# One batch of eight heads per unit, in place of four heads, in a cached-attention decode step beside an MLP

## The chip, the cores and the metric

The kernel runs on one core of one Trainium2 chip. The metric is the device time of one execution in microseconds (us), as a median over runs. A core has a matrix engine (TensorE, PE in the profile), a vector engine (VectorE, DVE), a scalar engine (ScalarE, ACT), GpSimd (POOL) and a queue engine (SyncE, SP) that here only issues transfers; 16 DMA engines carry every transfer. Tiles lie in SBUF, 128 partitions wide; TensorE writes its results to PSUM, from which VectorE or ScalarE copy them.

## The reference, cut to what matters

Eight batches, one query token each, width D = 448. Branch A is attention with 16 query heads over 8 cached key/value heads of width 256, on the last W = 1024 of 4096 cached rows; branch B is a layer norm and a two-layer MLP of width 1792. A sigmoid gate of x mixes them. All inputs are bfloat16.

```python
q = (x @ wq).reshape(B, Sq, Hq, Dh).transpose(0, 2, 1, 3)
k = jnp.repeat(k_cache[:, :, Sk - W:, :], rep, axis=1)      # rep = 2
v = jnp.repeat(v_cache[:, :, Sk - W:, :], rep, axis=1)
scores = jnp.einsum("bhqd,bhkd->bhqk", q, k) * (Dh ** -0.5)
o = jnp.einsum("bhqk,bhkd->bhqd", _softmax(scores), v)
a = o.transpose(0, 2, 1, 3).reshape(B, Sq, Hq * Dh) @ wo
h = _gelu(_layernorm(x) @ w1 + b1)
b = h @ w2 + b2
g = _sigmoid((x * gate_w).sum(-1, keepdims=True))
out = g * a + (1 - g) * b
```

The keys and values that are read make 33.6 MB each, `wq` and `wo` 3.7 MB each, `w1` and `w2` 1.6 MB each. Each byte is read once.

## The kernel before

**Units.** A unit is half a batch: four key/value heads, their eight query heads, 1024 rows, so 16 units (`NQ`). The keys of a unit are one 2 MB load into one slot of 16 KB per partition; so are its values.

**The plan of loads.** A list written out by hand (lines 151 to 172) gives the order of all large loads: the keys of unit 0 in two halves, `w1`, `wq` in two slots, `w2`, then keys and, three units behind (`LAG`), values in turn, and `wo` in two slots, whose last pieces are small (line 70). `pump` (95) issues them on SP's queue into a ring of nine slots (`RING`); `done` (101) frees a slot after the last matmul that reads it and issues the next load. A load also waits until the load eight before it has landed, since loads share eight semaphores.

**Order of the work.** No scheduler changes the order: every engine runs its instructions as the program lists them. For each unit `transpose_keys` (330) turns the keys on TensorE: 32 transposes of 128x128 words (two bfloat16 values moved as one float32), four to a PSUM tile of three buffers, each tile copied to SBUF in turn by ScalarE (349) or VectorE (351). Between these groups stand the softmax steps of the unit before (`steps`, 443): `expo` behind group 0, `turn` behind group 2, `bring` behind group 6. Then TensorE runs `values` of the unit three before (450), `scores` of this unit (391), VectorE takes the maximum (`top`, 405), and `finish` (476) of the unit three before follows.

- `scores` writes four heads to four strips of 32 partitions of `S_ps`; only eight rows of a strip are wanted, and of these two belong to the strip's own head.
- `expo` is the exponential with a row sum; `turn` a VectorE transpose of 32x32 blocks (423); `bring` two matmuls, one that permutes partitions (431) and one in float32 that spreads the sums (434).
- `values` multiplies two row chunks at a time into four strips of `PO`; VectorE adds the two chunks (465, 466).
- `finish` is two float32 matmuls (481) that add the strips, normalise and transpose at once, and a copy into `oT` (484).

**Ahead of the units** come the layer norm, the gate and their TensorE transposes (`norm_and_gate`, 272; `transposed`, 229), the MLP's first layer with the weights as the stationary operand (`mlp_hidden`, 488: 70 matmuls of eight columns), the queries (`query`, 356), and, after unit 0's scores, the second layer (`mlp_out`, 536: 60 matmuls of 112 columns in four strips). Small inputs come on ScalarE's queue (179 to 187), among them `gate_w` as a broadcast of eight rows and `b1` as 128 short rows.

**Behind the units**, `spread_rows` (584) moves the heads to the layout of `wo` with 32 small matmuls, `project` (599) multiplies with `wo` in 128 matmuls of 112 columns, one VectorE instruction (620) mixes the branches, and four DMAs, two on SP's and two on ScalarE's queue, write the output (630).

Of the kernel before, what the change touches and what calls it, by code (L numbers as in the profile page):

```python
# [17 lines left out]
def kernel(  # L18
# [15 lines left out]
    nc = tc.nc  # L34
# [10 lines left out]
    assert (NB, Sq, D, Hkv, Dh, Hq, W, F) == (8, 1, 448, 8, 256, 16, 1024, 1792)  # L45
    NJ = Dh // P
    NC = W // P
# [3 lines left out]
    NF = F // P  # L51
    FH = F // 2
    HH = HD // 2
    PAIR = 2
    OT = 4
    DO = D // OT
    QN = 512
    QUAD = 4
    RQ = QUAD * rep
    NQ = NB * Hkv // QUAD  # L60
    SK = P // QUAD
    NCK = W // SK
    NH = 2
    CH = NCK // NH
    SLOT = 8192
    CB = NC // NJ
    HPQ = 4
    NHQ = Hq // HPQ
    NJ8 = HPQ * NJ
    WO_PARTS = [[(0, NJ8)]] * (NHQ - 1) + [[(0, 4), (4, 6), (6, 8)]]  # L70
    RING = 9
    LAG = 3
    BIG = 1e30
# [8 lines left out]
    ktpool = ctx.enter_context(tc.tile_pool(name="ktpool", bufs=4))  # L82
    epool = ctx.enter_context(tc.tile_pool(name="epool", bufs=2))
    opool = ctx.enter_context(tc.tile_pool(name="opool", bufs=LAG + 1))
# [8 lines left out]
    consumed = [0]  # L93

# [10 lines left out]
    def kv_loader(src, u, parts):  # L105
        b, half = divmod(u, Hkv // QUAD)
        v = src[b, half * QUAD : (half + 1) * QUAD, kv_base:Sk, :].rearrange(
            "a (s c) d -> s a (c d)", c=NCK
        )

        def load(t):
            n = NCK * Dh // parts
            for i in range(parts):
                nc.sync.dma_start(  # L114
                    t[:, i * n : (i + 1) * n], v[:, :, i * n : (i + 1) * n]
                )

        return load

    def rows_loader(pieces):  # L120
        def load(t):
            o = 0
            for ap in pieces:
                n = 1
                for s in ap.shape[1:]:
                    n *= s
                dst = t[:, o : o + n]
                if len(ap.shape) == 3:
                    dst = dst.rearrange("p (a n) -> p a n", a=ap.shape[1])
                nc.sync.dma_start(dst, ap)  # L130
                o += n

        return load

    index = {}

    def add(key, loader):
        index[key] = len(plan)
        plan.append(loader)

    def add_kv(name, src, u, parts=1):
        add((name, u), kv_loader(src, u, parts))
# [5 lines left out]
    w2_v = B_w2.rearrange("(p c) n -> p (c n)", c=NF)  # L148
    wo_v = A_wo.rearrange("(q p j) n -> p q (j n)", p=P, j=NJ8)

    add_kv("k", A_k_cache, 0, parts=2)
    add(("w1",), rows_loader([w1_m, w1_t]))
    add(("wq", 0), rows_loader([wq_m[:, 0 : 2 * HD]]))
    add(("wq", 1), rows_loader([wq_m[:, 2 * HD : 3 * HD], wq_t]))
    add(("w2",), rows_loader([w2_v]))
    for u in range(1, NQ):
        add_kv("k", A_k_cache, u)
        if u >= LAG:
            add_kv("v", A_v_cache, u - LAG)
    for u in range(NQ - LAG, NQ):  # L160
        add_kv("v", A_v_cache, u)
    for q in range(0, NHQ, 2):
        add(
            ("wo", q),
            rows_loader(
                [
                    wo_v[:, q + i, j0 * D : j1 * D]
                    for i in range(2)
                    for j0, j1 in WO_PARTS[q + i]
                ]  # L170
            ),
        )

    def slot(*key):
        return slots[index[key]]

# [3 lines left out]
    gw_b = consts.tile([NB, D], BF16)  # L180
    b2_r = consts.tile([1, D], BF16)
    b1_sb = consts.tile([P, NF], BF16)
    nc.scalar.dma_start(
        gw_b[:], gate_w.rearrange("(o d) -> o d", o=1).to_broadcast([NB, D])
    )
    nc.scalar.dma_start(b2_r[:], B_b2.rearrange("(o d) -> o d", o=1))
    nc.scalar.dma_start(b1_sb[:], B_b1.rearrange("(p c) -> p c", c=NF))

# [4 lines left out]
    ones_f = consts.tile([P, P], F32)  # L193
    nc.gpsimd.memset(ones_f[:], 1.0)
# [3 lines left out]
    PO = ps_po.tile([P, PAIR, Dh], F32)  # L198
    nc.vector.memset(PO[:], 0.0)

    NX = NR + 2

    def tiles(ps):
        return [
            (ps[32 * i : 32 * i + NB, :], slice(i * DO, (i + 1) * DO))
            for i in range(OT)
        ]

    xz = consts.tile([NB, 2, P], BF16)
    yz = consts.tile([NB, 2, P], BF16)  # L210
    nc.vector.memset(xz[:], 0.0)
    nc.vector.memset(yz[:], 0.0)
    xT = consts.tile([P, NX, NB], BF16)
    yT = consts.tile([P, NX, NB], BF16)
    sel = consts.tile([P, RQ], F32)
    sel2 = consts.tile([P, RQ], F32)
    own = consts.tile([P, PAIR], F32)
    qw = consts.tile([P, NJ, NB, Hq // RQ, QUAD, RQ], BF16)
    oT = consts.tile([P, Hq, NJ, NB], BF16)
    gg = consts.tile([NB, 2], F32)  # L220
    spread = consts.tile([NB, OT, P // OT], F32)
    gg_s = consts.tile([P, 2], F32)
    ones_r = consts.tile([1, NB], BF16)
    mixb = consts.tile([P, DO], F32)
    res = consts.tile([P, DO], BF16)
    nc.vector.memset(spread[:], 0.0)
    nc.vector.memset(ones_r[:], 1.0)

    def transposed(dst, src, srcz):
        tp = ps_misc.tile([P, NX, NB], BF16, tag="misc", name="tp")  # L230
        for r in range(NR):
            nc.tensor.transpose(tp[:, r, :], src[:, r:DM:NR], ident[:NB, :NB])
        for h in range(2):
            nc.tensor.transpose(tp[:, NR + h, :], srcz[:, h, :], ident[:NB, :NB])
        nc.vector.tensor_copy(dst[:], tp[:])

    for h in range(2):
        nc.vector.tensor_copy(xz[:, h, h::2], x_sb[:, DM:D])
    transposed(xT, x_sb, xz)
    nc.vector.reduce_sum(  # L240
        sel[:], ident[:].rearrange("p (a s) -> p s a", a=QUAD)[:, 0:RQ, :], axis=AXIS.X
    )
    halfs = ident[:].rearrange("p (a s) -> p s a", a=QUAD)
    for i in range(PAIR):
        nc.vector.reduce_sum(
            own[:, i : i + 1], halfs[:, i * RQ : (i + 1) * RQ, :], axis=AXIS.XY
        )
    nc.vector.reduce_sum(
        sel2[:],
        ident[:]  # L250
        .rearrange("p (a h s) -> p s a h", a=QUAD, s=RQ)[:, :, :, 0:PAIR],
        axis=AXIS.XY,
    )
    perm = consts.tile([P, P], BF16)
    nc.vector.tensor_copy(
        perm[:].rearrange("p (s a) -> p s a", a=QUAD),
        ident[:].rearrange("p (a s) -> p s a", a=QUAD),
    )
    cap = consts.tile([P, 1], F32)
    rows = consts.tile([P, 1], F32)  # L260
    for a in range(QUAD):
        nc.vector.reduce_sum(
            rows[32 * a : 32 * a + 32, :],
            ident[32 * a : 32 * a + 32, (32 + rep) * a : (32 + rep) * a + rep],
            axis=AXIS.X,
        )
    nc.vector.tensor_scalar(
        cap[:], rows[:], 2.0 * BIG, -BIG, op0=ALU.mult, op1=ALU.add
    )
    nc.vector.memset(qw[:], 0.0)  # L270

    def norm_and_gate():
# [18 lines left out]
        for h in range(2):  # L291
            nc.vector.tensor_copy(yz[:, h, h::2], y_sb[:, DM:D])
        transposed(yT, y_sb, yz)
# [6 lines left out]
            in1=gw_b[:],  # L300
# [5 lines left out]
        nc.scalar.activation(gth[:], gl[:], ACT.Tanh, scale=0.5)  # L306
        nc.vector.tensor_scalar(
            gg[:, 0:1], gth[:], 0.5, 0.5, op0=ALU.mult, op1=ALU.add
        )
        nc.vector.tensor_scalar(  # L310
            gg[:, 1:2], gth[:], -0.5, 0.5, op0=ALU.mult, op1=ALU.add
        )
        nc.vector.tensor_copy(
            spread[:, :, 0:NB],
            ident[0:NB, 0:NB]
            .rearrange("p (o b) -> p o b", o=1)
            .to_broadcast([NB, OT, NB]),
        )
        gp = ps_misc.tile([P, 2], F32, tag="misc", name="gp")
        nc.tensor.matmul(  # L320
            gp[:],
            lhsT=spread[:].rearrange("p i b -> p (i b)"),
            rhs=gg[:],
# [3 lines left out]
        nc.vector.tensor_copy(gg_s[:], gp[:])  # L327

    KT = {}
    def transpose_keys(u, between=None):  # L330
        kn = slot("k", u)[:].bitcast(F32)
        between = between or {}
        for hf in range(NH):
            kt = ktpool.tile([P, QUAD, CH, SK, NJ], BF16, tag="kt", name="kt")
            KT[hf] = kt
            for i in range(CH // CB):
                c0 = i * CB
                g = hf * (CH // CB) + i
                ktp = ps_kt.tile([P, CB, P, NJ], BF16, tag="ktp", name="ktp")
# [12 lines left out]
                for step in between.get(g, ()):  # L352
                    step()
# [209 lines left out]
    for u in range(1, NQ):  # L563
        transpose_keys(u, steps(u - 1))
        if u >= LAG:
            values(u - LAG)
# [94 lines left out]
```

## Time and profile before

| | us |
|---|---|
| runs | 194.29, 194.04, 194.38 (median 194.29) |
| span of the profiled execution, first to last instruction | 192.9 |
| TensorE matmul busy | 141.4 (73%), 1478 matmuls and as many weight loads |
| VectorE busy | 121.4 (63%), 278 instructions |
| ScalarE busy | 84.3 (44%), 102 instructions |
| DMA | 77.90 MB in 6737 packets, mean 404 GB/s |
| mean granted TensorE clock | 0.907 |

How to read it. The profile is one execution; its span leaves out what lies around the first and last instruction, so the runs' median is 1.4 above it. The page cuts the span in 40 slices and gives each engine's busy share in tenths; PEclk is the clock granted to TensorE, and DMA the mean busy share of the 16 DMA engines. "The chain that ended last" goes back from the last instruction, at each step to what released it. A row of "groups" has the line, the engine, the operation, out<-in with shapes, the count, the busy time in all, the mean duration of one in ns, and the idle time of the engine before it with what ended most of that. A row of a timeline has start, duration, engine, line, operation, and in brackets the idle time before it and its releaser. A row of windows gives a stretch, its length, the busy time and count of PE, PEld (weight loads), DVE, ACT and POOL, then granted clock, DMA share and GB/s. Matmuls overlap, so the mean duration of one is more than the spacing between two.

### The profile page before, as it was taken

Reading aid. Unit: us, or ns where it says so; the run is one execution under the profiler, and the core shown is the slowest. Engines: PE = TensorE matmul, PEld = TensorE weight load, DVE = VectorE, ACT = ScalarE, POOL = GpSimd, SP = SyncE. Lnnn points to the kernel's source line nnn. Section 1 sums busy time; section 2 is a strip of 40 time slices with the busy share of each in tenths; the row PEclk is TensorE's granted clock in tenths of the full one; section 3 lists DMA queues with packets and bytes.
Section 4 is the critical chain, followed back from the end, with each engine's and each line's share of the span. In section 5 each row is a group of like instructions: output and inputs, shape, how many; then the busy total and the mean of one; then the engine's idle time right before and its main releaser. Section 6 shows DMA issues by size and latency. Waiting matters only on the chain.

```text
span 192.9 us, 3529 instructions
## 1 busy us (share of the span) xinstructions
PE 141.4 (73%) x1478; PEld 104.7 (54%) x1478; DVE 121.4 (63%) x278; ACT 84.3 (44%) x102; POOL 1.3 (1%) x9
## 2 busy tenths in 40 slices
PE   1299957788888859797858586869786978935671
PEld 0199526465575649484636363739473948612360
DVE  7632335797987848576858676765867584863310
ACT  2343024587583817182818182827282725520000
POOL 2000000000000000000000000000000000000000
PEclk9999699999999997969999999996999696995558
DMA  5999999999999999999999999999999999999960
GB/s 173 426 427 415 429 440 423 404 431 431 431 431 421 425 418 425 435 426 428 425 418 431 416 431 428 428 428 421 428 428 421 428 431 425 428 418 413 417 240 7
DMA packets 6737, 77.90 MB, mean 404 GB/s; under 512 B 945, under 2 KB 1346, under 8 KB 1986
## 3 DMA queue, kind: packets, MB, share of 16 engines
q1 hardware_dynamic: 6512, 77.67, 95.5%
q8 instruction: 11, 0.18, 0.4%
q10 hardware_dynamic: 210, 0.02, 0.2%
q14 instruction: 4, 0.03, 0.0%
HBM read 77.68 MB, written 0.01 MB: 403 GB/s over the span
## 4 chain that ended last, share of the span: by engine, by line
DMA 96%; SPq 1%; issue 0%; DVE 0%; PE 0%
DMA slot<-in_A_k_cache_dram 58%; DMA slot<-in_A_v_cache_dram 21%; DMA slot<-in_A_wo_dram 10%; DMA slot<-in_A_wq_dram 7%; SPq L114 1%; SPq L130 1%; DVE res L620 0%; PE A_ps L604 0%
## 5 line engine op out<-in xcount | busy, mean ns | idle before, releaser
L343 PE MATMUL ktp<-ident_f,slot 128*128 128x128 f32 x512 | 78.0, 306 | 24.3 <-DMA slot<-in_A_k_cache_dram 16.0
L349 ACT COPY kt<-ktp 128x1024 bf16<-128x1024 bf16 x64 | 63.2, 1016 | 71.2 <-PE ktp L343 71.1
L343 PEld LDWEIGHTS ktp<-ident_f,slot 128*128 128x128 f32 x512 | 64.7, 157 | 33.6 <-issue 16.2
L351 DVE COPY kt<-ktp 128x1024 bf16<-128x1024 bf16 x64 | 41.8, 686 | 27.5 <-PE ktp L343 27.5
L423 DVE STREAM_TRANSPOSE EB<-E 128x1024 bf16<-128x1024 bf16 x16 | 19.9, 1243 | 5.9 <-ACT E L415 5.9
L407 DVE TENSOR_REDUCE nmx<-S_ps 128x1 f32<-128x1024 f32 x16 | 19.5, 1219 | 3.3 <-PE S_ps L395 3.3
L456 PE MATMUL PO<-slot,ET 128*16 128x512 bf16 x256 | 18.3, 410 | 2.1 <-DMA slot<-in_A_v_cache_dram 2.1
L395 PE MATMUL S_ps<-kt,qw 128*8 128x512 bf16 x256 | 18.2, 388 | 1.4 <-ACT kt L349 1.1
L415 ACT ACTIVATE E<-S_ps,nmx 128x1024 bf16<-128x1024 f32 x16 | 17.9, 1119 | 2.4 <-DVE nmx L408 2.4
L395 PEld LDWEIGHTS <-qw 128*8 128x8 bf16 x256 | 7.1, 85 | 8.8 <-issue 2.1
L456 PEld LDWEIGHTS <-ET 128*16 128x16 bf16 x256 | 5.4, 91 | 8.7 <-issue 5.4
L436 DVE CAST ET<-sm 128x256 bf16<-128x256 f32 x16 | 6.6, 415 | 0.7 <-PE sm L434 0.7
L434 PEld LDWEIGHTS sm<-selr,ones_f 128*128 128x128 f32 x32 | 5.0, 198 | 0.6 <-issue 0.4
L484 DVE CAST oT<-sm 128x16 bf16<-128x16 f32 x16 | 3.5, 219 | 2.9 <-PE sm L481 2.9
L434 PE MATMUL sm<-selr,ones_f 128*128 128x8 f32 x32 | 4.8, 222 | 0.0
L431 PE MATMUL sm<-EB,perm 128*128 128x256 bf16 x16 | 4.5, 279 | 0.3 <-DVE oT L484 0.3
L604 PE MATMUL A_ps<-slot,oP 128*8 128x112 bf16 x128 | 3.5, 273 | 1.1 <-DMA slot<-in_A_wo_dram 1.1
L514 DVE TENSOR_TENSOR z<-hT,b_sb 128x112 f32<-128x112 f32 x1 | 0.3, 274 | 5.5 <-PE hT L504 5.5
L604 PEld LDWEIGHTS <-oP 128*8 128x8 bf16 x128 | 2.7, 114 | 1.8 <-issue 1.8
L415 ACT ACTIVATION_READ_ACCUMULATOR E<-S_ps,nmx 128x1 f32 x16 | 3.2, 202 | 0.0
L363 PE MATMUL S_ps<-slot,xT 128*8 128x512 bf16 x32 | 3.2, 576 | 0.0
L438 DVE RECIPROCAL rb<-sm 128x8 f32<-128x8 f32 x16 | 3.2, 198 | 0.0
(145 smaller groups left out, 82.5 us busy)
## 6 DMA issues: line engine op xcount, KB each, us to landing
slot<-in_A_v_cache_dram SPq DMA_DIRECT2D x16, 2048.0 KB, 38.1
slot<-in_A_k_cache_dram SPq DMA_DIRECT2D x15, 2048.0 KB, 37.5
slot<-in_A_wo_dram SPq DMA_DIRECT2D x3, 896.0 KB, 31.8
slot<-in_A_k_cache_dram SPq DMA_DIRECT2D x2, 1024.0 KB, 7.4
slot<-in_A_wq_dram SPq DMA_DIRECT2D x1, 2048.0 KB
slot<-in_B_w_dram SPq DMA_DIRECT2D x1, 1568.0 KB
slot<-in_B_w_dram SPq DMA_DIRECT2D x1, 1344.0 KB, 10.1
slot<-in_A_wq_dram SPq DMA_DIRECT2D x1, 1024.0 KB
```

The costliest lines, as they stand in the source:

```text
L343: nc.tensor.transpose(words[:, c, :, 0], kn[:, o : o + P], ident_f[:])
L349: nc.scalar.copy(dst, src)
L351: nc.vector.tensor_copy(dst, src)
L395: nc.tensor.matmul(S_ps[32 * a : 32 * a + RQ, hf * CH * SK : (hf + 1) * CH * SK], lhsT=qw[:, j, b, half, a, :], rhs=KT[hf][:, a, :, :, j], ...
L407: nc.vector.reduce_max(nmx[:], S_ps[:], axis=AXIS.X, negate=True)
L415: nc.scalar.activation(E[:], S_ps[:], ACT.Exp, bias=nmx[:], scale=1.0, accum_out=rowsum[:])
L423: nc.vector.transpose(EB[:].rearrange("p c r -> p (c r)"), E[:])
L431: nc.tensor.matmul(sm[:, 0:NCK, :], lhsT=perm[:], rhs=EB[:, :, 0:RQ], start=True, stop=True)
L434: nc.tensor.matmul(sm[:, NCK, :], lhsT=ones_f[:], rhs=selr[:], start=True, stop=True)
L436: nc.vector.tensor_copy(ET[:], sm[:, 0:NCK, :])
L456: nc.tensor.matmul(PO[32 * t : 32 * t + PAIR * RQ], lhsT=ET[:, PAIR * c : PAIR * (c + 1), :], rhs=vn[:, PAIR * c * Dh : PAIR * (c + 1) * D ...
L604: nc.tensor.matmul(dst, lhsT=oP[:, j, q, :], rhs=w[:, o + cols.start : o + cols.stop], start=(q == 0 and j == 0), stop=(q == NHQ - 1 and j ...
```

## The change

A unit becomes a whole batch: eight key/value heads, sixteen query heads. What follows from it:

- **Loads.** A slot holds 32 KB per partition and the ring four slots. Keys and values of a batch come as two 2 MB loads, heads 0 to 3 and 4 to 7. `wq` is one slot, `w1` and `w2` share one, `wo` is one. Order: keys 0, `wq`, `w1`/`w2`, keys 1, then values and keys in turn with values two places behind, values 6, values 7, `wo`.
- **Order of the work.** No softmax step stands between the transposes. A batch is `transpose_keys`, `scores`, `softmax`, `values` of the batch before, `bring`, `finish` of the batch before.
- **Scores.** The stationary operand has four columns, two heads' queries with zeros for the other, so that both halves of the batch add into one tile of 16 wanted rows.
- **Softmax.** The exponentials stay float32, the row sum is a 33rd block column, and one VectorE block turn of 1056 columns (397) brings both over. A stream shuffle copies the sums to all lanes of a block, a reciprocal and the gate follow, and one multiplication gives `EZ`. `bring` is one bfloat16 matmul; `ET` is spread with a mask.
- **Values.** 32 matmuls per batch; each reads a chunk of both halves.
- **Finish.** No matmuls: a block turn of 512 float32 columns out of PSUM and six small additions on VectorE write `oP` in the layout of `wo`.
- **Projections of x and y.** Transposes by VectorE block turns and copies. The activations are the stationary operand and the weights stream: 28 matmuls of 512 columns for the queries, 14 of 448 for the first MLP layer, which now comes after batch 0's softmax, and 14 of 448 for the second.
- **Small inputs.** `gate_w` and `b2` come as one row each, `b1` as four rows, in six DMAs of one row; stream shuffles spread them.
- **Output.** 16 projections of 448 columns, four additions into `acc`, 32 of 224 columns, three more additions, two output DMAs.

The built program has 2300 TensorE instructions for 2987. The bytes loaded are the same. Cut to its core, with the lines of the changed kernel:

```diff
-    RING = 9
-    LAG = 3
+    RING = 4                      # L69; SLOT = NG * HS, 32 KB per partition
+    EARLY = 16
...
+    add(("k", 0), kv_loader(A_k_cache, 0))                      # L141
+    add(("wq",), rows_loader([wq_m, wq_t]))
+    add(("w12",), rows_loader([w1_m, w1_t, w2_v]))
+    add(("k", 1), kv_loader(A_k_cache, 1))
+    for b in range(2, NB):
+        add(("v", b - 2), kv_loader(A_v_cache, b - 2))
+        add(("k", b), kv_loader(A_k_cache, b))
+    add(("v", NB - 2), kv_loader(A_v_cache, NB - 2))
+    add(("v", NB - 1), kv_loader(A_v_cache, NB - 1))
...
+    nc.scalar.dma_start(rows_r[0:1, 0, :], gate_w.rearrange("(o d) -> o d", o=1))
+    nc.scalar.dma_start(rows_r[0:1, 1, :], B_b2.rearrange("(o d) -> o d", o=1))
+    for t in range(QD):
+        nc.scalar.dma_start(
+            b1_r[BL * t : BL * t + 1, :],
+            B_b1[FQ * t : FQ * (t + 1)].rearrange("(o d) -> o d", o=1),
+        )
...
+    nc.vector.stream_shuffle(b1_b[:], b1_r[:], [0] * BL)        # L209
...
+        nc.vector.transpose(                                    # L243
+            xt[:].rearrange("p a i b -> p (a i b)"),
+            xs[:].rearrange("p a r d -> p (a r d)"),
+        )
...
+    def scores(b):                                              # L372
+        CQ = QN // SK
+        for n in range(W // QN):
+            for u in range(NG):
+                for j in range(NJ):
+                    for t in range(QD):
+                        nc.tensor.matmul(
+                            S_ps[BL * t : BL * t + UR, n * QN : (n + 1) * QN],
+                            lhsT=qw[:, j, b, t, rep * u : rep * u + UR],
+                            rhs=KT[u][:, t, n * CQ : (n + 1) * CQ, :, j],
...
+    def softmax(b):                                             # L389
+        nc.vector.reduce_max(nmx[:], S_ps[:], axis=AXIS.X, negate=True)
+        nc.scalar.activation(
+            E[:, 0:W], S_ps[:], ACT.Exp, bias=nmx[:], scale=1.0,
+            accum_out=E[:, W : W + 1],
+        )
+        nc.vector.transpose(EB[:].rearrange("p c r -> p (c r)"), E[:])
+        nc.vector.stream_shuffle(rs[:], EB[:, NCK, :], [0] * BL)
+        nc.vector.reciprocal(sc[:], rs[:, 0:UR])
+        nc.vector.tensor_scalar_mul(sc[:], sc[:], gall[:, b : b + 1])
+        nc.vector.tensor_tensor(EZ[:], EB[:, 0:NCK, 0:UR],
...
+    def bring(b):                                               # L412
+        nc.tensor.matmul(sm, lhsT=perm[:], rhs=EZ, start=True, stop=True)
+        nc.vector.tensor_tensor(ET, sm, mask, op=ALU.mult)
...
+    def values(b):                                              # L435
+        for c in range(NCK):
+            t = c % QD
+            nc.tensor.matmul(
+                PO[BL * t : BL * t + Hq],
+                lhsT=ET[:, c].rearrange("p u a r -> p (u a r)"),
+                rhs=vn[:, c],
...
+    def finish(b):                                              # L449
+        nc.vector.transpose(T[:], PO[:].rearrange("p u (e j) -> p u j e", j=J8))
+        for u in range(NG):
+            nc.vector.tensor_tensor(Y[:, :, u, :], T[0:64, ...], T[64:128, ...], op=ALU.add)
+        for i in range(QD):
+            nc.vector.tensor_tensor(oP[BL * i : BL * (i + 1), :, :, b], ..., op=ALU.add)
...
+    transpose_keys(0)                                           # L532
+    query()
+    scores(0)
+    softmax(0)
+    hs = mlp_hidden()
+    bring(0)
+    mlp_out(hs)
+    for b in range(1, NB):
+        transpose_keys(b)
+        scores(b)
+        softmax(b)
+        values(b - 1)
+        bring(b)
+        finish(b - 1)
...
+    values(NB - 1)
+    finish(NB - 1)
+    for c in range(EARLY):                                      # L555
+        nc.tensor.matmul(A1[BL * g : BL * g + NB, :], ...)
+    for g in range(QD):
+        nc.vector.tensor_tensor(acc[:], A1[BL * g : BL * g + NB, :], acc[:], op=ALU.add)
+    for c in range(EARLY, NCH):
+        mine, tile_, base = (side, A3, 2 * BL) if c in side else (main, A2, 0)
+        for h in range(2):
+            nc.tensor.matmul(tile_[base + BL * h : base + BL * h + NB, :], ...)
+        if c == side[-1]:
+            for h in range(2):
+                nc.vector.tensor_tensor(fin[BL * h : BL * h + NB, :], ..., op=ALU.add)
+    nc.vector.tensor_tensor(res, A2, fin, op=ALU.add)           # L589
+    nc.sync.dma_start(out_f[:, 0:HALF], res[0:NB, :])
+    nc.scalar.dma_start(out_f[:, HALF:D], res[BL : BL + NB, :])
```

## The prediction

> **What bounds the kernel now.** I read the page's slices first, then the chain that ended last, then the tail in order of time, then the rows of one batch.
>
> ```profile
> DMA  5999999999999999999999999999999999999960
> ...
> q8 instruction: 11, 0.18, 0.4%
> ...
> ## 4 chain that ended last, share of the span: by engine, by line
> DMA 96%; SPq 1%; issue 0%; DVE 0%; PE 0%
> ```
>
> The 16 DMA engines are full from slice 2 to slice 38, and 96% of the chain is loads: 77.9 MB set the end, and work on the engines counts only where it delays a load or lies behind the last one. The q8 line matters below: 11 packets of TensorE's own instructions, 16 KB each, ride on the same engines.
>
> The windows of the end (columns: stretch, length, busy per engine, granted clock, DMA share, GB/s):
>
> ```profile
> 184.00:185.00 1.00, 0.68 (x9) 0.69 (x13) 0.22 (x1) 0.00 (x0) 0.00 (x0) 0.50 1.02 396
> 185.00:186.00 1.00, 1.00 (x59) 1.00 (x61) 0.29 (x1) 0.00 (x0) 0.00 (x0) 0.50 0.70 267
> 186.00:187.00 1.00, 0.79 (x35) 0.54 (x24) 0.00 (x0) 0.00 (x0) 0.00 (x0) 0.50 0.46 162
> 187.00:188.00 1.00, 0.86 (x32) 0.72 (x32) 0.00 (x0) 0.00 (x0) 0.00 (x0) 0.62 0.14 52
> 188.00:189.00 1.00, 0.55 (x24) 0.36 (x24) 0.00 (x0) 0.00 (x0) 0.00 (x0) 1.00 0.05 20
> ```
>
> The share decays over 4 us: the engines do not finish together, and at 188.5 one of 16 is left. A load has landed only when its slowest engine has. The trace's semaphore increments (one per engine and load) show how this grew: 0.8 us between first and last engine at 20 us, 2.6 at 149, 3.4 at 155, 4.1 for the last values (176.4 to 180.5). Each instruction packet takes 1.03 to 1.23 us and its engine comes out about 1.6 us later. Packets 1 to 8 (20.7 to 133.8 us) each put back an engine that was at most 0.8 late; 9 and 10 (153.1, 169.2 us) hit engines already late, as if eight engines served them in turn.
>
> **Stream.** 2987 TensorE instructions made 11 packets, one per 272; 2300 make 8.5, so 8: no engine is hit twice, and the spread stays at 2.6. Further, the eight 896-byte rows of `gw_b` took 0.38 to 0.69 us on seven engines at 4.1 us, which is the 0.8 at the start; now it is one row. I take 2.2 at the end (between 1.8 and 2.6) for 4.15: 1.95 us earlier. The first keys come in rows of 16 KB at 0.614 us, not two of 8 KB at 0.32 each: 8 per engine, 0.2 us. Last values at 180.54 - 2.1 = 178.4, last `wo` piece at 189.40 - 2.1 = 187.3. Bytes stay the same.
>
> [...]
>
> **Tail.** Before, from the last values to the end:
>
> ```profile
> 180.54 1.89 PE L456 MATMUL PO<-slot,ET 128*16 128x512 bf16 x16 [0.23 <-DMA slot<-in_A_v_cache_dram]
> ...
> 189.40 0.27 PE L604 MATMUL A_ps<-slot,oP 128*8 128x112 bf16 x8 [0.31 <-DMA slot<-in_A_wo_dram]
> ...
> 189.72 0.33 DVE L620 SCALAR_TENSOR_TENSOR res<-A_ps,gg_s,mixb 128x112 bf16<-128x112 f32 x1 [4.07 <-PE A_ps L604]
> 190.09 0.71 SPq L630 DMA_DIRECT2D out_dram<-res  x2
> ```
>
> Now both halves of the batch wait for the last values. 32 matmuls at 1.89/16 are 3.8 at clock 0.50 (2.1 at full clock, from 1.04 for 16); I take 3.6, the clock returning near their end. `finish` on VectorE: block turn of 512 columns, scaled from 1.243 for 1024, 0.71; two adds of 64 and four of 32 by the 112-wide add's 0.274 (0.157 fixed, 0.117 streaming), with gaps 1.3: 2.0. First 16 projections 1.0. Four adds of 448 into `acc` at 0.62 + 0.04, each on the one before: 2.65. Two of 224 into `fin` 0.86, `res` 0.39. With 0.2 of handovers: 178.4 + 3.6 + 2.0 + 1.0 + 2.65 + 0.86 + 0.39 + 0.2 = 189.1, against 190.05: the VectorE adds, not the last load, end it. One output DMA per queue for two saves 0.36. Together -1.3. At full clock the last load binds, 187.3 + 0.4 + 0.39 = 188.1, so -2.3. The span is 192.9, the median 194.29, so 1.4 lies around the span; 193.0 to 192.0.
>
> **The chain of a batch.** Here the cover can go. Before, `expo`, `turn` and `bring` of one unit lay between the transposes of the next; now `softmax`, `bring`, `finish` stand in program order, and TensorE's next transposes wait behind `bring`, which waits for VectorE.
>
> ```profile
> L351 DVE COPY kt<-ktp 128x1024 bf16<-128x1024 bf16 x64 | 41.8, 686 | 27.5 <-PE ktp L343 27.5
> L423 DVE STREAM_TRANSPOSE EB<-E 128x1024 bf16<-128x1024 bf16 x16 | 19.9, 1243 | 5.9 <-ACT E L415 5.9
> L407 DVE TENSOR_REDUCE nmx<-S_ps 128x1 f32<-128x1024 f32 x16 | 19.5, 1219 | 3.3 <-PE S_ps L395 3.3
> L349 ACT COPY kt<-ktp 128x1024 bf16<-128x1024 bf16 x64 | 63.2, 1016 | 71.2 <-PE ktp L343 71.1
> L415 ACT ACTIVATE E<-S_ps,nmx 128x1024 bf16<-128x1024 f32 x16 | 17.9, 1119 | 2.4 <-DVE nmx L408 2.4
> ```
>
> One batch, from the first transpose. Sixteen groups of four transposes at 0.50, three PSUM buffers, ACT and VectorE evicting in turn (1.02, 0.69); VectorE's first eviction waits behind `ET` (512 wide, 0.69) and `finish` (2.0) until 2.65. Stepping the buffers gives 10.1. Scores 32 x 0.068 = 2.2, maximum 1.22, exp to the turn's start 1.24, turn of 1056 columns 1.28, four small operations 1.0 with gaps, `bring` and handovers 0.4: 17.4. TensorE rests 2.9 us in it behind `values`. What that does to the clock:
>
> ```profile
> 159.00:160.00 1.00, 0.00 (x0) 0.00 (x0) 0.00 (x0) 0.00 (x0) 0.00 (x0) 1.00 0.96 410
> 160.00:161.00 1.00, 0.90 (x6) 0.93 (x7) 0.00 (x0) 0.04 (x1) 0.00 (x0) 0.73 1.12 475
> 161.00:162.00 1.00, 1.00 (x7) 1.00 (x6) 0.24 (x1) 1.00 (x2) 0.00 (x0) 0.50 0.97 410
> ```
>
> After 1.94 us of rest the clock stood at 0.50 for 3 us, though at 90 to 130 us the same rest left it at 1.00. Half-clock transposes delay the fourth group by 0.3, the rest is hidden behind evictions: 17.7 at most, I take 17.5. A float32 turn, shuffles and a 72-row matmul have no row. If 4-byte turns took twice the bfloat16 row, the cycle would be 19.3; if the small operations overlapped, 17.0. I take the row's 1.28.
>
> [...]
>
> A batch's loads take 2 x 9.8 = 19.6 us (8.4 MB at 428 GB/s), so the engines catch up 2 us per batch, and must: they start late. VectorE reaches the first key evictions only after `norm_and_gate`, which now waits for the `b1` rows (six one-row DMAs, each packet taking turns with 0.61 us key packets: landing at 7 to 11 us) and turns 1280 columns (1.5): 16 to 20 us, for 11.7. Rest of `transpose_keys(0)` 8, query 3.5, scaling, turn and 32 copies into `qw` at 0.11 to 0.18, 6 to 8, scores and softmax 7, MLP 2.2 + VectorE 5.2 + 14 matmuls of 448 in one strip 3.3 to 4.9: batch 1 starts transposing at 52 to 58; I take 55. Batch 7's `ET` is then ready at 55 + 16.4 (no `finish` ahead in batch 1) + 6 x 17.5 + 1.0 = 177.4: just ahead of the values at 178.4. The `w1`/`w2` slot comes free at that start too; an issue needs 1.4 us to its first packet (0.73 to 2.16 at the beginning), and the 23.6 MB queued ahead run dry at 58.2 (as many had landed on the first engine of before at 58.7), so up to 56.8 the stream never stops. Slots of 4 MB otherwise come free 2 us or more ahead.
>
> **Rivals.**
> 1. The stream and the tail set the end (sum above): 192.9, own range 191.8 to 193.9. For: DMA at 1.00, catching up 2 us a batch. Chance 0.52.
> 2. Slower: the chain of a batch becomes the bound. It decides from the point where start + 16.4 + 6 cycles + 1.0 passes 178.4, 1 us from my sum; each 0.1 us of cycle then costs 0.6, each us of late start 1. Start 57.5, cycle 17.9: 182.3, so 3.9 over rival 1, 196.9. For: every step is serial, and VectorE's new forms are unmeasured. Against: 1.28 and 0.69 have close rows. Chance 0.31.
> 3. Fewer fetches do not shorten the stream, and only the longer tail is felt: values to `res` 10.7 for 9.5, less 0.36, +0.8: 195.1. Chance 0.09.
> 4. Rival 2 just begins and eats rival 1's gain: 194.3. Chance 0.08.
>
> **The numbers.** Rival 1's time is the forecast, 192.9. The range 191.7 to 197.5 reaches over rivals 1, 3, 4 and most of 2. Faster by over 0.2% (the smallest difference a measurement of this kernel tells from none): rival 1 and a share of 4, 0.54; within: 0.10; slower: 0.36.
>
> **What would show it.** Right: 8 instruction packets; last values within 2.6 us from first to last engine, landing near 178.4; `values` of batch 7 waiting for the load and not for `ET`; DMA share 1.00 throughout; VectorE's adds still running after the last piece's matmuls. Wrong: batch 7's key transposes starting past 163, or gaps in the DMA share near 58 to 70 (rival 2); 9 or more packets or a spread of 4 us (rival 3). A batch cycle above 18 would make the forecast wrong by itself.

## The result, and the profile after

| | before | after |
|---|---|---|
| median of runs, us | 194.18 (4 runs beside it) | 205.43 (205.16 to 206.17, 4 runs) |
| ratio after/before | | 1.0584 (95%: 1.0562 to 1.0605) |
| span of the profiled execution | 192.9 | 203.2 (its own time 205.16) |
| DMA mean, GB/s | 404 | 383 |
| mean granted TensorE clock | 0.907 | 0.863 |

The change made the kernel 5.8% slower; 192.9 had been forecast. The page of the kernel after, its slices, the instruction queue and the chain that ended last:

```profile
DMA  6999999999944999999999999999999999999700
...
q8 instruction: 9, 0.15, 0.3%
...
PE 36%; DVE 35%; ACT 19%; DMA 4%; issue 4%; ACTq 1%; DVEq 0%
```

Before, the DMA share was 9 from slice 2 to slice 38 and loads made 96% of the chain. Now the DMA line has a hole in its twelfth and thirteenth slices, and DMA makes 4% of the chain, all of it the small `b1` rows at the start: TensorE, VectorE and ScalarE, each waiting for the one before, set the end. The windows around the hole (stretch, length, busy time of PE, PEld, DVE, ACT, POOL, clock, DMA share, GB/s):

```profile
57.00:58.00 1.00, 0.00 (x0) 0.00 (x0) 0.97 (x3) 0.00 (x0) 0.00 (x0) 0.50 0.85 360
58.00:59.00 1.00, 0.97 (x3) 0.35 (x4) 0.57 (x1) 0.00 (x0) 0.00 (x0) 0.50 0.08 33
...
63.00:64.00 1.00, 1.00 (x10) 1.00 (x11) 0.59 (x2) 0.44 (x1) 0.00 (x0) 1.00 0.00 0
```

The queued loads run dry at 58, as the prediction had worked out (58.2), and almost nothing moves until 64. SP's timeline shows what ends it, and the table of SP's waits (us in total, times, longest us) what it waited for:

```profile
30.93 1.18 SPq L115 DMA_DIRECT2D slot<-in_A_k_cache_dram  x2
62.97 1.18 SPq L115 DMA_DIRECT2D slot<-in_A_v_cache_dram  x2
```
```profile
SPq L115 <- PE bb L522: 30.8, 1, 30.8
```

Between the two issues SP waits 30.8 us for `bb` (line 522): values 1 go into the slot of `w1`/`w2`, which the second MLP layer releases at 62.9. The chain in order of time (start, duration) shows why so late:

```profile
30.94 4.71 ACT qs L349
...
50.34 1.29 PE hp L475 x9
...
58.02 4.91 PE bb L522 x14
```

The query scaling, batch 0's scores and softmax (to 49.8), then the first and the second MLP layer stand one behind the other. At 62.9 batch 1's key transposes begin as well (TensorE's timeline):

```profile
62.87 1.53 PE L310 MATMUL ktp<-ident_f,slot 128*128 128x128 f32 x12
```

From there the chain runs without waiting for a load to its end:

```profile
187.97 0.69 DVE ET L423
188.66 0.63 DVE T L451
...
189.34 3.24 PE PO L440 x24
```

The last values had landed on their slowest engine at 184.96; their matmuls start at 189.34, behind `ET` of batch 7 and behind the block turn that empties `PO` of batch 6. So there are two delays that overlap: the stream is 6.6 to 7 us late (184.96, for the 178.4 forecast and the 177.9 to 178.1 of the runs below that have no hole), and the chain of batches another 4.4 behind the stream.

### The profile page after: what moved, and what is told of

Read it like the earlier page. It is cut to its first block, busy times and chain, and to the rows that moved or that the text cites. A ratio compares the mean times of both kernels' runs of the same rounds, so it can differ in the third digit from the quotient of the medians.

```text
span 203.2 us, 2811 instructions
## 1 busy us (share of the span) xinstructions
PE 126.4 (62%) x1136; PEld 86.7 (43%) x1136; DVE 121.6 (60%) x277; ACT 81.6 (40%) x86; POOL 2.5 (1%) x12
## 4 chain that ended last, share of the span: by engine, by line
PE 36%; DVE 35%; ACT 19%; DMA 4%; issue 4%; ACTq 1%; DVEq 0%
PE ktp L310 19%; ACT kt L316 12%; PE S_ps L378 9%; DVE EB L397 5%; DVE nmx L391 5%; ACT E L392 4%; DMA b_r<-in_B_b_dram 4%; DVE oP L461 4%; PE bb L522 2%; ACT qs L349 2%; DVE T L451 2%; DVE ET L423 2%; DVE qw L370 2%; DVE kt L318 2%; PE PO L440 2%
## 5 line engine op out<-in xcount | busy, mean ns | idle before, releaser
L310 PE MATMUL ktp<-ident_f,slot 128*128 128x128 f32 x512 | 80.2, 316 | 24.3 <-ACT kt L316 10.1
L378 PE MATMUL S_ps<-kt,qw 128*4 128x512 bf16 x256 | 17.8, 418 | 10.2 <-DVE qw L370 10.2
L392 ACT ACTIVATE E<-S_ps,nmx 128x1024 f32<-128x1024 f32 x8 | 8.9, 1114 | 31.5 <-DVE nmx L391 31.5
L391 DVE TENSOR_REDUCE nmx<-S_ps 128x1 f32<-128x1024 f32 x8 | 9.8, 1225 | 11.7 <-PE S_ps L378 11.7
L397 DVE STREAM_TRANSPOSE EB<-E 128x1056 f32<-128x1056 f32 x8 | 10.2, 1278 | 10.7 <-ACT E L392 10.7
L378 PEld LDWEIGHTS <-qw 128*4 128x4 bf16 x256 | 6.5, 85 | 18.4 <-issue 11.8
L440 PEld LDWEIGHTS <-ET 128*16 128x16 bf16 x256 | 7.5, 94 | 12.3 <-DVE ET L423 4.2
L461 DVE TENSOR_TENSOR oP<-Y 32x32 bf16<-32x32 f32 x32 | 9.4, 294 | 1.1
L522 PE MATMUL bb<-slot,hs 128*8 128x448 bf16 x14 | 4.9, 534 | 5.4 <-DVE hs L509 5.4
L423 DVE TENSOR_TENSOR ET<-sm,mask 128x512 bf16<-128x512 f32 x8 | 5.5, 691 | 2.2 <-PE sm L415 2.2
L451 DVE STREAM_TRANSPOSE T<-PO 128x512 f32<-128x512 f32 x8 | 5.7, 707 | 1.2 <-PE PO L440 1.2
L349 ACT ACTIVATE qs<-S_ps 128x1024 bf16<-128x1024 f32 x1 | 4.7, 4703 | 2.1 <-PE S_ps L339 2.1
```

The costliest lines, as they stand in the source:

```text
L310: nc.tensor.transpose(words[:, c, :, 0], kn[:, o : o + P], ident_f[:])
L378: nc.tensor.matmul(S_ps[BL * t : BL * t + UR, n * QN : (n + 1) * QN], lhsT=qw[:, j, b, t, rep * u : rep * u + UR], rhs=KT[u][:, t, n * CQ ...
L391: nc.vector.reduce_max(nmx[:], S_ps[:], axis=AXIS.X, negate=True)
L392: nc.scalar.activation(E[:, 0:W], S_ps[:], ACT.Exp, bias=nmx[:], scale=1.0, accum_out=E[:, W : W + 1],)
L397: nc.vector.transpose(EB[:].rearrange("p c r -> p (c r)"), E[:])
L423: nc.vector.tensor_tensor(ET[:].rearrange("p c u a r -> p (c u) a r"), sm[:] .rearrange("p k (o r) -> p k o r", o=1) .to_broadcast([P, NCK ...
```

## The experiments

Theory 1: the chain of batches starts too late (62.9 for the forecast's 55), and this is the loss. Theory 2: the batch cycle is too long by itself. All kernels are edits of the kernel after; ratios are to the kernel before on the same chip.

**MLP moved (a_mlp_early).**

```diff
     transpose_keys(0)
     query()
-    (query scaling, turn and copies, in query)
-    scores(0); softmax(0)
-    hs = mlp_hidden(); bring(0); mlp_out(hs)
+    qs = query_scale()
+    hs = mlp_hidden(*mlp_first())
+    query_turn(qs)
+    mlp_out(hs)
+    scores(0); softmax(0); bring(0)
```

> One edit on the changed kernel: the first MLP layer follows the query matmuls, its VectorE work lies beside ScalarE's 4.70 us query scaling, the second layer beside the copies into qw; so the w1/w2 slot is freed near 44 us and not at 62.9. Theory 1 (the late start of the batch chain is the loss: batch 1's key transposes began at 62.9, where the prediction had 55, and behind it everything is serial): those transposes start near 53.6, the DMA share stays at 1.00 from 56 to 66 us, batch 7's ET is ready near 179.4 instead of 188.66, and the time is 195.9 (194.5 to 197.5). Theory 2 (the batch cycle of 18.0 us against the 17.5 predicted is the loss): the start does not matter, and the time stays above 203.

Measured: 195.64 (ratio 1.0078, 1.0051 to 1.0105), span 194.0. The transposes of batch 1 start near 51, the DMA share has no hole, the last values land at 178.1, `ET` of batch 7 starts at 178.91. The cycles from batch 2 on are as long as before (17.9 to 19.2). Theory 1 holds; theory 2 had said above 203. Moving 13 us of work that nobody needed early, and that held a slot, gives back 9.8.

**The start trimmed (b_start).**

```diff
-    nc.vector.stream_shuffle(b1_b[:], b1_r[:], [0] * BL)   # L209; now at its use, ahead of L495
         nc.scalar.activation(
-            qs[:].rearrange("p m j e -> p m e j"),
-            S_ps[:].rearrange("p (m e j) -> p m e j", e=BL, j=NJ),
+            qs[:],
+            S_ps[:].rearrange("p (m e j) -> p m j e", e=BL, j=NJ),
```

> Two edits on the changed kernel, the MLP stays where it is: the b1 shuffle moves to its first use, so that VectorE does not wait for the b1 rows until 11.28 us (3.3 us earlier), and the query scaling writes contiguously and reads PSUM with a stride (if the scattered 2-byte writes made it 4.70 us, it takes about 1.0, as the contiguous one of the kernel before). Theory 1: batch 1's transposes start near 55.9, the w1/w2 slot is freed just before the loads run dry, no gap in the DMA share, time 198.2 (197 to 199.5); if the scaling stays at 4.70, start 59.6 and 201.9. Theory 2 (cycle): above 203.

Measured: 197.77 (1.021, 1.0151 to 1.0269), no hole in the DMA share, start at 53.8. The scaling, first row of the kernel after, second of this one (operation, count | busy, mean ns):

```profile
L349 ACT ACTIVATE qs<-S_ps 128x1024 bf16<-128x1024 f32 x1 | 4.7, 4703 | 2.1 <-PE S_ps L339 2.1
```
```profile
L347 ACT ACTIVATE qs<-S_ps 128x1024 bf16<-128x1024 f32 x1 | 1.0, 1024 | 1.9 <-PE S_ps L337 1.9
```

The same elements cost 4.70 or 1.02 us by which side has the stride: it was the 2-byte writes 64 bytes apart, not the read of PSUM. Two small edits, with the MLP where it was, are worth 7.7 us.

**finish earlier (c_finish_early).**

```diff
         softmax(b)            # maximum and exponential
         values(b - 1)
+        finish(b - 1)
+        softmax_rest(b)       # turn to EZ
         bring(b)
-        finish(b - 1)
```

> One edit on the changed kernel: finish of the batch before stands between the maximum and the block turn, beside ScalarE's exponential, and no longer between ET and the next key evictions. The cycle falls from 18.0 to about 16.8; the start (62.9) and the gap in the loads from 58.8 to 64 stay. Theory 1: the chain catches up until the late values of batch 7 (landing 184.6) bind, then 3.3 for values and 10.6 to the end: span 198.5, time 200.4 (199.5 to 201.5). If the gap in the loads cost nothing by itself, 198. Theory 2: 205.4 - 6 x 1.2 = 198.2 or less.

Measured: 211.83 (1.0945, 1.0871 to 1.102): a miss, 11 us above what was expected. The cycles are 18.7 to 19.6. VectorE's rows:

```profile
93.59 0.72 DVE L453 STREAM_TRANSPOSE T<-PO 128x512 f32<-128x512 f32 x1 [0.50 <-PE PO L442]
...
96.15 1.28 DVE L399 STREAM_TRANSPOSE EB<-E 128x1056 f32<-128x1056 f32 x1
```

From maximum to `ET` it takes 6.95 for 5.23: `finish` first waits 0.5 for the matmuls of `values`, then holds the turn 1.7 past the end of the exponential (94.4 to 96.15). From `ET` to the next maximum only 1.0 is won. And TensorE now rests 4.97 us for 3.25, behind which the granted clock stood at 0.50 for 3.4 us in one cycle and 6.8 in the next. The expectation had forgotten the wait on `values`, and counted `finish` behind `ET` at its full length.

**finish spread out (k_spread).**

```diff
                     nc.vector.tensor_copy(dst, src)     # L318, key evictions
+                    if todo:
+                        todo.pop(0)()                   # one of the six additions
...
-        finish(b - 1)
+        finish(b - 1, now=(b == NB - 1))                # only the block turn at once
```

> The changed kernel with finish taken apart: its block turn stays behind ET, its six small additions follow one each behind VectorE's next six key evictions, in the 0.2 to 0.65 us that VectorE waits there. Start (62.9) and tail stay. If the 3.2 us that ET and finish hold VectorE ahead of its first eviction make the cycle 17.9 at full clock (TensorE waits 1.62 us for that eviction, line 318), the cycle falls by 1.3 to 1.6, batch 7's ET is ready near 180, its values (landing near 184 behind the gap in the loads) bind, time 200.7 (199.8 to 202). If finish is hidden, 204 or more.

Measured: 200.80 (1.0338, 1.0289 to 1.0386). TensorE's transposes of one batch, first in the kernel after, then here:

```profile
134.07 0.66 PE L310 MATMUL ktp<-ident_f,slot 128*128 128x128 f32 x4 [0.28 <-ACT kt L316]
136.35 1.53 PE L310 MATMUL ktp<-ident_f,slot 128*128 128x128 f32 x12 [1.62 <-DVE kt L318]
```
```profile
111.30 10.07 PE L310 MATMUL ktp<-ident_f,slot 128*128 128x128 f32 x64
```

The 1.62 us stall is gone, the 64 transposes run through, and six cycles take 17.07 each (from 18.16 in the mean). Now `ET` of batch 7 is there at 180.45, and the chain shows the last values, landing at 183.4, as what the end waits for. So the hole in the loads had its price too, hidden until then behind the chain: 183.4 against 178.1 in the kernels without the hole. Not all of the 4.6 us is the edit's: batch 1's transposes began at 61.15 in this execution, 1.7 before those of the kernel after, though nothing was edited ahead of them (0.9 lie ahead of batch 0's scores, 0.8 in the second MLP layer, 4.09 for 4.91). The six cycles alone are 6.5 shorter. So theory 2 has a share too: both the start and the cycle hold the chain back.

**Narrow second layer and output (d_narrow).** The edit: 112 columns in four strips, as in the kernel before, for the second MLP layer and the output projection; one VectorE addition for seven.

> The second MLP layer (14 matmuls of 448 columns, 4.91 us) and the output projection (16 of 448, 32 of 224 and seven VectorE additions) go back to 112 columns in four strips, 56 and 128 matmuls, with one addition at the end and four output DMAs; the rest of the changed kernel stays. If strips run beside each other, the MLP layer takes about 2.0, so the chain starts 2.7 earlier (60.2), and the tail behind the last oP is 4.5 instead of 5.5: time 201.7 (200.5 to 202.8). If width does not matter, 204.4 to 205.5. One more instruction packet (10 for 9).

Measured: 203.59 (1.0484, 1.041 to 1.0559; runs from 202.09 to 205.08), span 203.0 in the profile. From `hs` to the end of the second layer it takes 2.3 for 4.9 us, as expected, and from the last turn of `PO` to the output DMA 4.7 for 8.1, over three times the gain that was expected there. But the six cycles of this execution, the slowest of the four, are 18.3 to 19.4, with stretches of 6.8 us at a clock of 0.50, and add 4.1 to their sum, so that its span gains 0.2. The narrow forms are shorter in their own rows; what they are worth in the sum this run leaves open, and f_tail below measures it for the output.

**A busy TensorE in its rest (h_warm).** 32 matmuls of 64 columns per batch between `values` and `bring`, results unread.

> The changed kernel with 32 matmuls of 128 x 64 (result never read) per batch in TensorE's rest of 3.25 us between values and bring, nothing else changed. If the granted clock of 0.50 behind that rest is what makes the cycles 17.5 to 19.2 (mean 18.2), the clock stays at 1.00 there and the cycles are 17.2 to 17.5: batch 7's ET ready near 183.7, its values (landing 184.6) bind, time 200.7 (200 to 201.5). If the cold stretch is hidden behind the evictions, as the prediction had it (0.1 per cycle), 205.

Measured: 203.98 (1.0513, 1.0477 to 1.0549). The rest shrinks only to 2.2 us (32 such matmuls take 1.11), three of six cycles still have the clock at 0.50, for 3.4, 6.8 and 3.4 us (17.8, 19.3 and 19.0), the other three stay at 1.00 and take 17.9. Their sum is not shorter than in the kernel after; what was gained lay at the start, where nothing was edited. Inconclusive on how to hold the clock; but it shows 17.9 as the cycle at full clock.

**All start edits (e_start_all).** a_mlp_early and b_start together.

> The three start edits together (first MLP layer beside the query scaling, b1 shuffle at its first use, contiguous scaling). Theory 1: with the start out of the way the chain meets the loads: it now waits for the keys of each batch, batch 7's keys land near 158.4, its ET is ready at 176.4 to 177.6, just ahead of its values (178.0), and from there 13.7 to the end as in the run with the MLP moved alone: span 191.9, time 193.6 (193.0 to 194.6), no different from the kernel before or a little less. Theory 2 (the batch cycle is a bound of its own): no gain on the 195.64 of the run with the MLP moved alone.

Measured: 194.66 (1.0017, 1.0005 to 1.0028). The batch chain starts at 46.4; `ET` of batch 7 starts at 177.26, the values land at 178.1 and their matmuls begin at 178.63, behind the block turn of `PO`. The time came as expected, but not by the way that was expected, so its fit is in part luck: the chain does not wait for keys. TensorE's only wait for a key load is the one at the start (us in total, times, longest us):

```profile
PE ktp L308 <- DMA slot<-in_A_k_cache_dram: 8.6, 1, 8.6
```

It comes close (batch 7's keys have landed at 158.52, its transposes start at 158.67). Of the 4.5 us that the start gains on a_mlp_early only 1.7 reach `ET` of batch 7, since the cycles here take 17.9 to 19.4 (18.8 in the mean), five of the six with 6.8 us at a clock of 0.50. From the last values on it is as forecast: the tail ends it.

**The tail (f_tail).** e_start_all, and the output as 128 matmuls of 112 columns:

```diff
-    for c in range(EARLY): ...          # 16 matmuls of 448 columns, four additions into acc
-    for c in range(EARLY, NCH): ...     # 32 of 224, two additions into fin, one into res
+    for c in range(NCH):
+        for t in range(QD):
+            o = c * D + t * DO
+            nc.tensor.matmul(A[BL * t : BL * t + NB, :], lhsT=oP[:, c % J8, c // J8, :],
+                             rhs=w[:, o : o + DO], start=(c == 0), stop=(c == NCH - 1))
+    nc.vector.tensor_tensor(res[:], A[:], acc[:], op=ALU.add)
```

> As the run with the three start edits, and the output projection in 128 matmuls of 112 columns in four strips with one VectorE addition and four output DMAs, as in the kernel before; the second MLP layer stays 14 wide matmuls. The chain behind the last values ends near 186.6, before the last wo piece (186.9), so the last load binds: 186.9 + 0.3 + 0.35 + 2.9 = span 190.5, time 192.1 (191.6 to 193.0), 1.1% less than the kernel before. If the additions were not what ended the tail, 193.6 as without this edit.

Measured: **192.47 (0.9909, 0.9895 to 0.9924)**: 0.9% below the kernel before, a small gain, but its interval leaves out 1, and some 6% below the kernel after. Its chain at the end:

```profile
148.63 29.24 DMA slot<-in_A_v_cache_dram
...
178.00 3.61 PE PO L442 x29
```

The values' matmuls start as the load lands: last values at 177.87, 2.6 ahead of the kernel before (180.50), last `wo` piece at 186.69. The end hangs on a load again, but on the last values and not, as expected, on the last `wo` piece: the chain behind the values reaches the final addition at 187.44, 0.75 after that piece has landed.

**More instructions (g_more_instr).** f_tail and 48 small unread matmuls per batch.

> As f_tail, with 48 small matmuls (128 x 32, result never read) per batch in TensorE's rest between values and bring, 336 in all: 672 more TensorE instructions, 11 or 12 instruction packets for 9. Left as it is: all that is computed. If each packet puts back an engine that is never idle and an engine that is hit twice ends later (the stream step of the prediction), the last values are spread over 3 to 4 us instead of 2 and the time is 1.0 to 2.0 above f_tail. If instruction packets are hidden, the same time as f_tail, or less by a warmer clock.

Measured: 193.70 (0.9975, 0.9965 to 0.9984), 1.23 above f_tail. Twelve instruction packets for nine; in both the first engine finishes the last values at 175.8, the last one at 177.87 in f_tail and at 179.10 here. The semaphore increments of the sixteen engines show which: in f_tail seven engines end by 176.42 and nine between 177.34 and 177.87; here thirteen have ended by 177.88 and exactly three, as many as there are packets more, at 179.04 to 179.10. The stream step of the prediction holds.

**Half the values early (i_half), a warm end (j_warm_end), both (l_both_end).** f_tail, with batch 7's values in two halves; with 8 unread matmuls of 448 columns ahead of them; with both.

> As f_tail; batch 7's values go in two halves of 32 matmuls of 256 columns, the first as soon as heads 0 to 3 have landed (2.2 us ahead of the rest). In f_tail the chain behind the last values (3.61 at a clock of 0.50, then 6.1 to the sum) ends 0.7 us behind the last wo piece (186.7). With one half done early it ends near 185.2, and the last wo piece binds: 186.7 + 0.3 + 0.35 + 2.75 = span 190.1, time 192.1 (191.8 to 192.4). If the first half waits for both loads, 192.5 as f_tail.

> As f_tail, with 8 matmuls of 448 columns (result never read) ahead of batch 7's values, in TensorE's rest of 3 us. If they bring the clock to 1.00, values take 2.1 for 3.61 and the projection 1.8 for 3.19, and the last wo piece binds: time 192.1. If the clock stays at 0.50, they take 3.4 us themselves and values start 0.5 late: 192.5 to 193.0.

> Both edits of the end together: the last wo piece binds in any case, 192.1 (191.8 to 192.4); less than that would say that the span behind the last load (0.3 + 0.35 + 2.75) was mis-sized.

Measured: 193.53 (0.9968, 0.9954 to 0.9983), 192.35 (0.9908, 0.9892 to 0.9924) and 193.58 (0.998, 0.9962 to 0.9998). In j_warm_end the clock, already at 0.50, stays there and nothing changes. i_half misses its 192.1 for a reason that confirms the stream step: 32 more matmuls move an instruction packet from 186.02 to 181.70, into the `wo` pieces. The chain that ended last in i_half:

```profile
168.02 19.85 DMA slot<-in_A_wo_dram
187.87 0.04 issue
187.92 0.38 PE A L596 x8
```

The last piece lands at 187.87 for 186.69, 1.18 us later by one packet: fifteen engines have ended it by 186.59, one ends at 187.87. The values were indeed earlier (second half done at 180.1, for 181.6 in f_tail), which bought nothing. l_both_end misses its 192.1 in the same way: a packet at 183.75, the last piece at 188.04.

## Why the prediction was wrong, point by point

**The failed step is the start of batch 1's transposes in "The chain of a batch": "batch 1 starts transposing at 52 to 58; I take 55".** It took 62.9. Even the upper ends of its terms add to only 58.8; what lay beyond them was the scaling, the scores and the MLP, in the middle of the chain, not the beginning, which had looked uncertain:

| term | forecast | measured |
|---|---|---|
| `norm_and_gate` done | 16 to 20 | 20.0 |
| rest of `transpose_keys(0)` | 8 | 8.5 |
| query | 3.5 | 2.4 |
| scaling, turn, 32 copies | 6 to 8 | 10.1 |
| scores and softmax | 7 | 8.7 |
| MLP | 10.7 to 12.3 | 13.1 |

- *Scaling*: counted at about 1 us by the row of the kernel before (1.02), while the rearranged output made it 4.70. b_start shows the whole difference. The diff showed the output pattern; it was not priced.
- *Scores* took 3.81 for 2.2: TensorE had rested 10.15 us and the clock stood at 0.50.
- *MLP*: its 14 one-strip matmuls at half clock were at the upper end (4.9), and it waited 0.5 more behind `softmax`, since its memset stands behind `EZ` on VectorE.

**The cycle, 17.5.** Warm it is 17.9, and 18.16 in the mean. The 17.5 counted VectorE held by `ET` and `finish` for 2.65 us; it is 3.3 (132.29, first transpose, to 135.60, first eviction), and the stall it makes is the 1.62 shown above. k_spread removes it. The rows that the prediction called unmeasured were right: the turn of 1056 float32 columns took 1.28, the small operations 1.0.

**The clock.** "The rest is hidden behind evictions: 17.7 at most" came near where the clock stood at 0.50 for 3.4 us (18.0 with it at 113.5 to 116.9, 17.9 in the next cycle without it), and failed where it lasted 6.8 (19.2 at 151.1 to 157.9, 18.4 at 168.1 to 175.0). The clock fell in four of the five cycles from 91 to 188 us, each with a rest of about 3.25 (3.23 to 3.25 ahead of `bring`, line 415). The traces show why the same rest does both. Their clock records change only on a grid of 3.41 us, and what a step brings goes with how long matmuls ran in the step before. In the kernel after (windows: the second and third figures are the length and PE's busy time, the clock is third from the end):

```profile
127.15:130.56 3.41, 1.79 (x36) 0.79 (x25) 1.96 (x2) 1.21 (x2) 0.00 (x0) 1.00 0.98 413
130.56:133.98 3.42, 1.60 (x13) 1.29 (x12) 2.93 (x9) 0.97 (x2) 0.00 (x0) 1.00 1.01 431
147.63:151.04 3.41, 0.94 (x9) 0.87 (x9) 2.84 (x8) 0.19 (x2) 0.00 (x0) 1.00 1.03 437
151.04:154.46 3.42, 2.26 (x12) 1.66 (x10) 3.18 (x10) 1.91 (x2) 0.00 (x0) 0.50 0.98 417
154.46:157.87 3.41, 3.41 (x17) 3.41 (x17) 1.04 (x2) 1.76 (x2) 0.00 (x0) 0.50 1.03 437
```

The rest of 128.9 to 132.2 is split by the grid (1.79 and 1.60 us busy), and the clock stays; that of 146.9 to 150.1 falls mostly into one step (0.94), and the next step runs at 0.50; with 2.26 us busy in it the one after does too, and after 3.41 the clock is back. Over all fourteen traces, of the steps at full clock the 109 with under 1.4 us of matmuls were all followed by 0.50 and 324 of the 325 with over 2.0 by full clock (between, both occur); of the steps at 0.50 all 107 with under 2.5 were followed by 0.50 and all 112 with over 2.6 by full clock. In the two traces of before and after alone, from their first clock records on (13.7 and 24.8 us), it is 11 of 11, 53 of 54, 10 of 10 and 16 of 16. So it is the busy time in a step that goes with the clock, not the length of the rest; the drop behind 1.94 us in the kernel before, on which the prediction leaned, fits as well (1.26 us busy in the step of 157.04 to 160.45). This is read from the traces; no run was made to test it.

**Rival 2 was right as a mechanism**, "the batch chain becomes the bound ... each us of late start 1", and too small: with start 62.9 its own formula gives 62.9 + 16.4 + 105 + 1.0 = 185.3; the six cycles were 4.0 longer in all and the other terms 0.6 shorter, which makes the measured 188.66. It did not count that the block turn of batch 6's `finish` stands between `ET` and the last values (0.68). Its warning signs came, gaps near 58 to 70 and batch 7's transposes past 163 (169.4), and so did a cycle above 18; its chance of 0.31 was too low, since every term of the start was serial and taken near its middle.

**Stream.** Right, and measured apart from the delay: where nothing holds the loads, the last values land at 177.9 to 178.1 (forecast 178.4) and the last `wo` piece at 186.6 to 187.0 (187.3). The spread between the engines is 2.0 to 2.3 (forecast 2.2) for 4.2 before. The packets' part was tested; the parts of the `gw_b` rows and of the first keys were not taken apart. Nine packets came, not eight, but the ninth only at the last landing or behind it (186.02 in f_tail, 196.28 in the kernel after). g_more_instr and i_half show what packets cost that fall on engines which never rest (a mean DMA share of 0.99 from 170 to 184 us in i_half): the last values land 1.23 us later in the one, the last `wo` piece 1.18 us later in the other.

**Tail.** Values to `res` were 3.6 + 7.1 in the forecast and 3.24 + 8.1 measured: `finish` 2.55 for 2.0, the first 16 projections 1.48 for 1.0. "VectorE adds, not the last load, end it" held, and f_tail shows the price: 2.2 us less, of which 1.4 lie behind the start of the last values in the two traces and 0.6 are an earlier start.

**Time around the span.** Taken as 1.4 from two different executions; within one execution it is 1.7 to 1.95 in the kernel before and 1.9 to 2.0 in the kernel after. That alone is 0.5.

Together, from the forecast's 178.4 for the last values: `ET` of batch 7 is ready 10.3 later, the turn of `PO` adds 0.7, the tail 0.6 (-0.4 and +1.0), the rest 0.2, which is the span's 203.2 against 191.5.

## What to carry to other kernels

When work is regrouped into larger units, follow the first unit from its first DMA to the release of each slot, every term at the duration of its own access pattern: this chain had to catch up 2.1 us per unit to be just in time (19.6 for the loads, 17.5 forecast), caught up 1.4, and could not repair a start 8 us late as well. Work that no one needs early but that holds a slot (here an MLP of 13 us) goes beside a wait, not into the chain. And where the transfer engines never rest, count the instruction packets that share them, above all those near the last load.

## What the runs showed that was not expected

- ScalarE's copy of 128x1024 float32 to bfloat16 takes 4.70 us with its writes 64 bytes apart (kernel after) and 1.02 with contiguous writes and the read strided instead (b_start). No run here tries a stride between.
- One instruction packet near the end moved the last landing by 1.18 us (i_half), so that a kernel with a shorter chain ended later.
- The stretch at a clock of 0.50 behind the same rest of 3.25 us lasted 0, 3.4 or 6.8 us in successive cycles of one execution (the kernel after), by how the rest fell on a grid of 3.41 us. 1.1 us of small matmuls in that rest (h_warm) did not always prevent it: the steps ahead of the drops still had only 1.2 to 1.5 us of matmuls. 3.2 us of them at the end (j_warm_end) did not bring the clock back, as they fell on two steps with 2.2 and 2.4 us busy.
- Three packets more left exactly three of the sixteen engines 1.2 us behind the others at the last values (g_more_instr).
